# A copy later in ScalarE's queue, fewer warming matmuls, full-height transposes and a narrower update in a linear-attention and two-MoE kernel

## The chip, the cores and the metric

The kernel runs on one core of a Trainium2 chip. The metric is device time in microseconds (us) for one launch. Before the change three runs took 834.9, 834.96 and 835.65 us; the median is 834.96 us.

## What is computed

Three stages follow one another, all in float32 as far as the result can see.

```
state[d,e] = alpha[t,d] * state[d,e] + k[t,d] * v[t,e]     # linear attention with decay, 4 x 8 heads,
y[t,e]     = sum_d q[t,d] * state[d,e]                     # 768 steps, head size 48
x  = y as 3072 tokens x 384
h  = x @ w_in;  x1 = (h * cos(h)) @ w_out                  # first MoE: hidden size 2048
e  = argmax(x1 @ w_gate)                                   # second MoE: 8 experts, hidden size 1024
out[token] = softmax weight * sigmoid(x1 @ w_output_gate)[e] * (relu(x1 @ w1[e]) @ w2[e])
```

## The kernel before

**Attention.** Time is cut into 6 chunks of 128 steps. A unit `u` is one chunk of one batch (`u % 4` is the batch, `u // 4` the chunk), 24 units in all; its 8 heads are kept as 4 pairs. For each unit VectorE (DVE) scans the decays (`decay`, L143, and `recip`, L152), DVE and GpSimd (POOL) scale queries and keys, TensorE (PE) makes scores (L200), transposes the keys (`k_trans`, L211, copied by ScalarE, ACT, in `keys`, L224), applies them to the values (L250, L258) and computes what the chunk adds to the state (`update`, L272; added in `update_out`, L287 and L289). `update` has one matmul for each of the 4 pairs: 112 stationary columns, and 128 moving columns, of which only the first 48 and the last 48 hold values; the 32 between them are zeros of the layout. The profile shows each of these float32 matmuls as two instructions, so 8 for a unit. The units of the last chunk have no update.

**Carry.** `carry(u)` does two things. DVE multiplies the decay total of the chunk before (`wtot`) into `dc` (L184), and then ACT copies the new total into `wtot` (L186). That copy must come after the multiplication, as it overwrites what the multiplication reads. `wtot` of a batch is next read by that batch's next unit, four units on.

**First MoE.** Tokens are handled in 6 groups of 512 (four units each). Each group has 16 blocks of 128 hidden columns; a slot `J` is one block of one group, 96 slots in all. In a slot PE runs `stage1` (9 matmuls, L366), then attention work of other units, then `stage2` of the block two slots earlier (9 matmuls, L405). Between them the block passes ACT `nearest` (L373), DVE `turn` (L379), ACT (L380, L381), DVE `gated` (L384), ACT (L391) and POOL (L392). In the first 16 slots the weights are also unpacked: DVE `narrow` (L334, L339, L343), then ACT and POOL `halves` (L354, L355).

**Order.** All engines run their instructions strictly in the order in which the program writes them. The order is written out by hand: every slot has places A, T, B, P, C and D, and a table says which attention step stands at which place. Place A comes right behind `stage1` and ahead of `nearest`; place C stands behind `stage2`. `carry(u)` stands at place A of slot J+2, ahead of `halves` and `nearest`. Units 5, 6 and 7 have theirs in slots 3, 6 and 9; units 8 to 23 have theirs from slot 17 on. Units 0 to 4 are prepared ahead of the slots, where `carry` is simply written last.

**Start.** While the first loads come in, `warm(22)` gives PE 22 matmuls on a zero tile (L717); `warm(9)` comes later, between the first key transposes and the first values. Both stand in PE's queue ahead of the real work.

**Second MoE.** The rows are sent to buckets by expert in memory and fetched back 448 at a time: three tiles of 128 rows and one of 64 (the first 256 rows of expert 0 are done early, which leaves it 128 and 64). `load_rows` fetches them and sets 10 columns of the 64 missing rows to zero on DVE (L617). `rows_trans` transposes each tile on PE in three pieces of 128 columns (L629), ACT and DVE copy the result out (L630, L631). Experts 1 to 7 take 12 transposes each, in the order 128, 128, 128, 64 rows, three times; it stands among the matmuls of the expert before (L658). In all there are 24 transposes of 64 rows.

Of the kernel before, what the change touches and what calls it, by code (L numbers as in the profile page):

```python
# [8 lines left out]
F32 = mybir.dt.float32  # L9
# [10 lines left out]
B, H, S, D = 4, 8, 768, 48  # L20
DM = H * D
KD = DM // 128
C = 128
# [14 lines left out]
ROW = DM + 10  # L38

QO, KO, AO, VO = 0, 4 * C, 8 * C, 8 * C + 4 * 130 + 8  # L40
UCOL = VO + 4 * C
EARLY = 256
MAGIC = 1.5 * 2.0 ** 23
TWO_PI = 2.0 * math.pi
# [10 lines left out]
def kernel(  # L55
# [11 lines left out]
    nc = tc.nc  # L67
# [6 lines left out]
    ps_a = ctx.enter_context(tc.tile_pool(name="ps_a", bufs=1, space=PSUM))  # L74
    ps_h = ctx.enter_context(tc.tile_pool(name="ps_h", bufs=2, space=PSUM))
    ps_m = ctx.enter_context(tc.tile_pool(name="ps_m", bufs=3, space=PSUM))
# [9 lines left out]
    x_p = m1.enter_context(tc.tile_pool(name="x_p", bufs=1, side="left"))  # L86
# [4 lines left out]
    u_p = at.enter_context(tc.tile_pool(name="u_p", bufs=3, side="right"))  # L91
# [12 lines left out]
    ident = c_sb[:, CI:CI + 128]  # L104
# [7 lines left out]
    wtot = [st_p.tile([128, 4], F32, name=f"wtot{b}") for b in range(B)]  # L112


    un, wt, rc, sc_t, y_t, xt = {}, {}, {}, {}, {}, {}

    def load_unit(u, parts=((0, UCOL),)):
        if u not in un:
            if u == B - 1:

                un[u] = tuple(x_p.tile([128, n], F32, tag=t, name="un") for n, t in ((AO, "xh"), (UCOL - AO, "xl")))
            else:
                t = u_p.tile([128, UCOL], F32, tag="un", name="un")
                un[u] = (t[:, 0:AO], t[:, AO:UCOL], t)
        for c0, c1 in parts:
            t, o = (un[u][2], 0) if len(un[u]) > 2 else (un[u][c0 // AO], c0 // AO * AO)
            nc.sync.dma_start(out=t[:, c0 - o:c1 - o], in_=units[u][:, c0:c1])

    def views(u):
        qk, av = un[u][:2]  # L130
        return (
            qk[:, QO:QO + 4 * C].rearrange("p (a c) -> p a c", a=4),
            qk[:, KO:KO + 4 * C].rearrange("p (a c) -> p a c", a=4),
            wt[u],
            av[:, VO - AO:].rearrange("p (a c) -> p a c", a=4),
        )

    def decay(u):
# [38 lines left out]
    def carry(u):  # L177

        b, i = u % B, u // B
        w = views(u)[2]  # L180
        wb = wtot[b].rearrange("p (a c) -> p a c", c=1)
        if i > 0:
            dc_t[u] = d_p.tile([128, 4, 1], F32, tag="dc", name="dc")
            nc.vector.tensor_tensor(out=dc_t[u], in0=wb, in1=w[:, :, 64:65], op=ALU.mult)  # L184
        if i < NCH - 1:
            nc.scalar.copy(wb, w[:, :, 129:130])  # L186

    def carry_state(u, eng=nc.gpsimd):
        b, i = u % B, u // B
        if i > 0:  # L190
            dc = dc_t.pop(u)
            m = state[b]
            eng.tensor_tensor(out=m, in0=m, in1=dc.to_broadcast([128, 4, 2 * D]), op=ALU.mult)
# [72 lines left out]
    def update(u):  # L266
        if u // B == NCH - 1:
            return
        ks = sc_t[u][1]
        pp = (ps_a if u < B else ps_m).tile([128, 4, C], F32, tag="acc1" if u < B else "m", name="pp")  # L270
        for p in range(4):
            nc.tensor.matmul(  # L272
                out=pp[0:64 + D, p, :], lhsT=ks[:, p, :], rhs=views(u)[3][:, p, :],
                start=True, stop=True,
            )
        pp_t[u] = pp

    def update_out(u):
        b, i = u % B, u // B
        if i == NCH - 1:  # L280
            return
        pp = pp_t.pop(u)
        for p0, c0, v0 in ((0, 0, 0), (64, D, C - D)):
            m = state[b][p0:p0 + D, :, c0:c0 + D]
            pv = pp[p0:p0 + D, :, v0:v0 + D]
            if i == 0:
                nc.scalar.copy(m, pv)  # L287
            else:
                nc.vector.tensor_tensor(out=m, in0=pv, in1=m, op=ALU.add)  # L289
# [316 lines left out]
    def load_rows(e, r0, n, pool, tag):  # L606

        tiles = [min(128, n - o) for o in range(0, n, 128)]
        nt = len(tiles)
        xe = pool.tile([128, nt, ROW], F32, tag=tag, name="xe")  # L610
        full, rest = divmod(n, 128)
        r0 += e * REG
        after_sends(nc.sync.dma_start(
            out=xe[:, 0:full, :], in_=xs[r0:r0 + full * 128, :].rearrange("(j p) c -> p j c", p=128)
        ))
        if rest:
            nc.vector.memset(xe[rest:128, full, DM:ROW], 0.0)  # L617
            after_sends(nc.sync.dma_start(out=xe[0:rest, full, :], in_=xs[r0 + full * 128:r0 + n, :]))
        return dict(e=e, n=n, tiles=tiles, xe=xe)

    def rows_trans(r, pool, th, tl):
        n = r["n"]
        xh = pool.tile([128, KD, n], F32R, tag=th, name="exh")
        xl = pool.tile([128, KD, n], F32R, tag=tl, name="exl")
        for k in range(KD):
            tp = ps_m.tile([128, 512], F32, tag="m", name="tp")[:, :n]
            for j, m in enumerate(r["tiles"]):
                o = j * 128
                nc.tensor.transpose(tp[:, o:o + m], r["xe"][0:m, j, k * 128:(k + 1) * 128], ident[0:m, 0:m])  # L629
            nc.scalar.copy(xh[:, k, :], tp)  # L630
            nc.vector.tensor_tensor(out=xl[:, k, :], in0=tp, in1=xh[:, k, :].bitcast(F32), op=ALU.subtract)  # L631
        r["x"] = (xh, xl)
        r["h"] = {}
# [80 lines left out]
    def warm(n):  # L714
        idle = ps_h.tile([128, 512], F32, tag="h", name="idle")
        for _ in range(n):
            nc.tensor.matmul(out=idle, lhsT=busy[:, 0:128], rhs=busy, start=True, stop=True)  # L717
# [5 lines left out]
    def at_slot(J, place, f, *args):  # L723
        plan.setdefault((J, place), []).append(lambda: f(*args))
# [6 lines left out]
    for u in range(GU, NU):  # L731
        J = NF * (u // GU - 1) + ((-2, 1, 4, 7) if u // GU == 1 else (-1, 2, 5, 7))[u % GU]
        at_unit[u] = J
        if u > GU:

            at_slot(max(J - 6, at_unit[u - 3] + 7 if u - 3 >= GU else 0), "A", load_unit, u)
            at_slot(J, "A", decay, u)
            at_slot(J, "D", q_right, u)
            at_slot(J, "B", recip, u)
            at_slot(J + 1, "D", q_left, u)  # L740
            at_slot(J + 2, "A", k_left, u, nc.vector)
            at_slot(J + 2, "A", k_right, u, nc.vector)
            at_slot(J + 2, "A", carry, u)
            at_slot(J + 2, "D", carry_state, u)
        at_slot(J + 3, "P", scores, u)
        at_slot(J + 3, "C", masked, u, 0)
        at_slot(J + 4, "A", masked, u, 1)
        at_slot(J + 4, "P", k_trans, u)
        at_slot(J + 4, "C", keys, u)
        at_slot(J + 5, "P", values, u)  # L750
        at_slot(J + 5, "C", x_out, u)
        at_slot(J + 6, "P", update, u)
        at_slot(J + 6, "C", update_out, u)
    for g in range(NG - 1):
        J = NF * (g + 1)

        fi = (2, 2, 3)
        tr, n, rn, sd = ((2, 3, 4, 4), 7, 9, 10) if g < NG - 2 else ((2, 3, 4, 5), 5, 7, 8)
# [30 lines left out]

    with tc.manual_schedule():  # L790
        nc.scalar.activation(out=busy[:, 0:1], in_=halfpi, func=ACTF.Sin)
        warm(22)
        load_words(0, 0)
        load_words(0, 1)
        load_words(0, 2)
# [3 lines left out]
        def prepare(u):  # L799
            if u == 0:  # L800
                decay(u)
            q_right(u)
            k_left(u, nc.gpsimd)
            recip(u)
            k_right(u, nc.vector)
            q_left(u, nc.vector)
            carry(u)

        prepare(0)
        scores(0)  # L810
# [46 lines left out]
        k_left(4, nc.vector)  # L857
        k_right(4, nc.vector)
        carry(4)
        carry_state(4, nc.vector)  # L860
        nc.vector.tensor_copy(base, c_sb[:, CEB:CEB + E])
        nc.vector.tensor_copy(tri16, c_sb[:, CT:CT + 128])
# [5 lines left out]
        for J in range(NF * NG):  # L868
            g, j = divmod(J, NF)
# [17 lines left out]
            t = nearest(g, j)  # L887
# [14 lines left out]
    with tc.manual_schedule(engines={ENG.PE, ENG.Activation, ENG.DVE, ENG.SP}):  # L902
# [60 lines left out]
        r = begin(0)  # L963
        rows_trans(r, z_p, "exh", "exl")
        second(7)
        for t in range(n_t):
# [7 lines left out]
            out=nt[:, 0:E], in0=nt[:, 0:E], scalar1=float(127 - CAP), scalar2=127.0, op0=ALU.add, op1=ALU.max  # L974
# [5 lines left out]
        for e in range(E):  # L980
# [8 lines left out]
            for j in range(NEF):  # L989

                n = r["n"]
# [28 lines left out]
            r = nxt  # L1020
# [6 lines left out]
    with tc.If(nov > 0):  # L1027
        with tc.tile_pool(name="ov_p", bufs=1, side="left") as ov_p:
# [13 lines left out]
            for e in range(E):  # L1042
# [6 lines left out]
                with tc.For_i(0, n_e, 1) as it:  # L1049
# [3 lines left out]
                        out=far, in0=far, scalar=float(E * REG), in1=rid, op0=ALU.mult, op1=ALU.add  # L1053
# [4 lines left out]
                        out=xs, out_offset=bass.IndirectOffsetOnAxis(ap=ri, axis=0),  # L1058
# [4 lines left out]
                    tp = ps_m.tile([128, KD, C], F32, tag="m", name="tp")  # L1063
# [3 lines left out]
                    for j in range(NEF):  # L1067
                        hp = ps_h.tile([128, 512], F32, tag="h", name="hp")[:, :C]
                        for k in range(KD):
                            nc.tensor.matmul(  # L1070
                                out=hp, lhsT=f1[:, k, j * 128:(j + 1) * 128], rhs=xT[:, k, :],
# [4 lines left out]
                    for j in range(NEF):  # L1076
                        nc.tensor.matmul(
                            out=op, lhsT=hT[:, j, :], rhs=f2[:, j, :], start=(j == 0), stop=(j == NEF - 1)
# [3 lines left out]
                        out=out, out_offset=bass.IndirectOffsetOnAxis(ap=tk[:, 0, :], axis=0),  # L1082
# [75 lines left out]
```

## Time and profile before

| what | value |
|---|---|
| median of three runs | 834.96 us |
| profiled execution, its own time | 836.24 us |
| its span | 834.5 us |
| granted TensorE clock, mean | 0.987 |
| PE busy | 797.1 us (96%) |
| DVE busy | 500.4 us (60%) |
| ACT busy | 427.3 us (51%) |
| POOL busy | 311.4 us (37%) |

Span and rows are from one profiled execution. A line of a timeline begins with the start and the length in us, then the engine, the line of the kernel, the operation, what it writes and reads, and how many instructions were merged; the bracket at the end is how long the engine stood idle before it and what it waited for. PEld is the load of TensorE's stationary operand, which overlaps with the matmuls. The granted clock is 1.00 at 2.4 GHz and 0.50 at 1.2 GHz.

### The profile page before, as it was taken

What the parts mean: (1) busy time and instruction counts of PE and PEld (TensorE: products, weight loads), DVE (VectorE), ACT (ScalarE), POOL (GpSimd) and SP (SyncE); (2) the same over time, 40 slices, a digit from 0 to 9 for tenths busy, and PEclk for the clock granted to TensorE, in tenths of its full rate; (3) what the DMA queues carried; (4) which work ended last, traced back from release to release, by engine and by line L of the source; (5) the groups of instructions that cost most, each with busy time, mean ns of one, the idle gap of its engine ahead of it and who ended that gap; (6) DMA issues with size and microseconds to landing.
All of it is one profiled execution on the core that took longest, in us unless ns stands there. A gap on an engine that the chain in (4) does not pass through costs nothing.

```text
span 834.5 us, 13942 instructions
## 1 busy us (share of the span) xinstructions
PE 797.1 (96%) x5415; PEld 671.7 (80%) x5415; DVE 500.4 (60%) x968; ACT 427.3 (51%) x782; POOL 311.4 (37%) x284
## 2 busy tenths in 40 slices
PE   8679799999999999999999999999999999999994
PEld 4457577788888888888878878889999999999994
DVE  7989998675467546763766335653764464454530
ACT  2355455754575457644665476564554453453420
POOL 3456557544355336443555333742000100101101
PEclk9998999999999999999999999999999999999998
DMA  9424443723201130123010002304753543533201
GB/s 336 162 98 165 165 165 105 256 59 113 73 2 52 71 122 0 52 70 123 1 52 30 30 1 77 115 1 146 232 160 104 166 140 110 167 123 117 78 11 36
DMA packets 46731, 85.22 MB, mean 102 GB/s; under 512 B 4136, under 2 KB 38216, under 8 KB 44096
## 3 DMA queue, kind: packets, MB, share of 16 engines
q1 hardware_dynamic: 43200, 74.67, 27.5%
q0 software_dynamic: 3456, 9.57, 3.1%
q8 instruction: 45, 0.74, 0.4%
q14 instruction: 30, 0.25, 0.1%
HBM read 69.01 MB, written 15.99 MB: 102 GB/s over the span
## 4 chain that ended last, share of the span: by engine, by line
PE 53%; issue 27%; DVE 10%; POOL 4%; ACT 2%; DMA 1%; POOLq 0%; SPq 0%; ACTq 0%; DVEq 0%
PE acc L405 21%; PE hp L366 21%; POOL out_dram L678 4%; DVE cv L334 2%; PE sc L200 2%; DVE cv L339 2%; PE yp L258 2%; PE yp L250 2%; PE pp L272 1%; DVE cv L343 1%; PE tp L429 1%; DVE t L384 1%; DVE w L143 1%; DVE t L379 1%; PE lp L461 1%
## 5 line engine op out<-in xcount | busy, mean ns | idle before, releaser
L392 POOL TENSOR_TENSOR gl<-t,gh 128x512 fp32r<-128x512 f32 x95 | 126.8, 1335 | 182.3 <-ACT gh L391 140.2
L373 ACT ACTIVATE t<-hp 128x512 f32<-128x512 f32 x96 | 57.3, 597 | 121.5 <-PE hp L366 110.6
L384 DVE TENSOR_TENSOR t<-hp,t 128x512 f32<-128x512 f32 x96 | 65.7, 684 | 88.1 <-ACT t L381 88.1
L379 DVE SCALAR_TENSOR_TENSOR t<-t,hp 128x512 f32<-128x512 f32 x96 | 65.7, 685 | 86.9 <-ACT t L373 86.6
L678 POOL DMA_INDIRECT out_dram<-ot,tk x32 | 30.9, 967 | 220.8 <-ACT ot L677 220.5
L658 PE MATMUL op<-h,hb 128*128 128x384 f32 x384 | 102.8, 340 | 0.0
L648 DVE SCALAR_TENSOR_TENSOR hb<-hp,hb 128x64 fp32r<-128x64 f32 (+3 forms) x136 | 45.3, 372 | 75.4 <-ACT hb L646 75.3
L405 PE MATMUL acc<-gh,woh 128*128 128x512 f32 x288 | 89.1, 416 | 0.0
L366 PE MATMUL hp<-xh,wih 128*128 128x512 f32 x288 | 84.3, 401 | 4.7 <-DVE t L384 2.9
L405 PE MATMUL acc<-gl,woh 128*128 128x512 f32 x288 | 84.4, 400 | 0.0
L405 PE MATMUL acc<-gh,wol 128*128 128x512 f32 x288 | 83.8, 399 | 0.0
L366 PE MATMUL hp<-xh,wil 128*128 128x512 f32 x288 | 83.5, 398 | 0.0
L366 PE MATMUL hp<-xl,wih 128*128 128x512 f32 x288 | 83.4, 398 | 0.0
L380 ACT ACTIVATE t<-t 128x512 f32<-128x512 f32 x96 | 60.7, 632 | 34.8 <-DVE t L379 34.8
L586 DVE TENSOR_TENSOR l<-raw,h 128x768 fp32r<-128x768 f32 x60 | 57.3, 957 | 32.5 <-ACT h L582 31.1
L646 ACT ACTIVATE hb<-hp 128x448 fp32r<-128x448 f32 (+2 forms) x72 | 36.3, 504 | 71.6 <-PE hp L644 71.5
L381 ACT ACTIVATE t<-t,halfpi 128x512 f32<-128x512 f32 x96 | 69.6, 725 | 3.1
L658 PEld LDWEIGHTS op<-h,hb 128*128 128x128 f32 x384 | 69.9, 188 | 0.5
L366 PEld LDWEIGHTS hp<-xh,wih 128*128 128x128 f32 x288 | 54.1, 190 | 19.6 <-DVE t L384 2.0
L366 PEld LDWEIGHTS hp<-xl,wih 128*128 128x128 f32 x288 | 54.7, 190 | 13.4
L405 PEld LDWEIGHTS acc<-gl,woh 128*128 128x128 f32 x288 | 54.7, 190 | 13.2
L366 PEld LDWEIGHTS hp<-xh,wil 128*128 128x128 f32 x288 | 54.5, 189 | 13.2
(139 smaller groups left out, 1501.6 us busy)
## 6 DMA issues: line engine op xcount, KB each, us to landing
raw<-in_w_dram SPq DMA_DIRECT2D x64, 384.0 KB, 3.2
un<-in_units_dram SPq DMA_DIRECT2D x20, 1032.0 KB, 5.1
raw<-in_w_in_dram SPq DMA_DIRECT2D x16, 384.0 KB, 3.6
raw<-in_w_out_dram SPq DMA_DIRECT2D x16, 384.0 KB, 4.0
xs<-zrow SPq DMA_DIRECT2D x8, 591.0 KB, 5.9
xe<-xs SPq DMA_DIRECT2D x7, 591.0 KB, 5.6
un<-in_units_dram SPq DMA_DIRECT2D x4, 512.0 KB, 6.0
un<-in_units_dram SPq DMA_DIRECT2D x4, 264.0 KB, 5.1
```

What stands on the lines that cost most here:

```text
L366: nc.tensor.matmul(out=hp, lhsT=w[:, k, fs], rhs=x[:, k, :], start=(n == 0), stop=(n == 3 * KD - 1))
L373: nc.scalar.activation(out=t, in_=hps[g, j], func=ACTF.Copy, bias=MAGIC)
L379: nc.vector.scalar_tensor_tensor(out=t, in0=t, scalar=MAGIC, in1=hp, op0=ALU.subtract, op1=ALU.subtract)
L380: nc.scalar.activation(out=t, in_=t, func=ACTF.Abs)
L381: nc.scalar.activation(out=t, in_=t, func=ACTF.Sin, scale=-TWO_PI, bias=halfpi)
L384: nc.vector.tensor_tensor(out=t, in0=hps.pop((g, j)), in1=t, op=ALU.mult)
L392: eng.tensor_tensor(out=gl, in0=gf, in1=gh.bitcast(F32), op=ALU.subtract)
L405: nc.tensor.matmul(out=acc[g][k], lhsT=w[:, j, ks], rhs=a, start=(j == 0 and n == 0), stop=(j == NF - 1 and n == 2),)
L586: (nc.vector.tensor_tensor if i < 4 else sub)(out=lo, in0=raws[i], in1=h.bitcast(F32), op=ALU.subtract)
L648: nc.vector.scalar_tensor_tensor(out=out_, in0=hp[:, c], scalar=0.0, in1=hh[:, c].bitcast(F32), op0=ALU.max, op1=ALU.subtract)
L658: nc.tensor.matmul(out=op, lhsT=a[:, sl], rhs=w[:, j, :], start=(j == 0 and i == 0), stop=(j == NEF - 1 and i == 2))
L678: sent = nc.gpsimd.indirect_dma_start(out=out, out_offset=bass.IndirectOffsetOnAxis(ap=tk[0:n, t, :], axis=0), in_=ot[0:n], in_offset=None ...
```

## The change

Four edits in one step.

1. The ACT copy of the decay total leaves `carry` and becomes `carry_keep`, which stands at place C of the same slot. Ahead of the slots it is still written right behind `carry`.
2. `warm(22)` becomes `warm(17)`.
3. `rows_trans` transposes all tiles with all 128 rows and a 128-column identity, and `load_rows` sets the 64 missing rows to zero over all 394 columns.
4. `update` moves only the 96 columns that hold values, by a strided view of two runs of 48; its result is 96 columns wide, and the unit's tile is 32 columns longer so that the view of the last pair stays inside.

```diff
+UPAD = UCOL + C - 2 * D
...
         if i > 0:
             dc_t[u] = d_p.tile([128, 4, 1], F32, tag="dc", name="dc")
             nc.vector.tensor_tensor(out=dc_t[u], in0=wb, in1=w[:, :, 64:65], op=ALU.mult)
+
+    def carry_keep(u):
+        b, i = u % B, u // B
         if i < NCH - 1:
-            nc.scalar.copy(wb, w[:, :, 129:130])
+            nc.scalar.copy(wtot[b].rearrange("p (a c) -> p a c", c=1), views(u)[2][:, :, 129:130])
...
-        pp = (ps_a if u < B else ps_m).tile([128, 4, C], F32, tag="acc1" if u < B else "m", name="pp")
+        pp = (ps_a if u < B else ps_m).tile([128, 4, 2 * D], F32, tag="acc1" if u < B else "m", name="pp")
         for p in range(4):
+            o = VO - AO + p * C
+            v = un[u][1][:, o:o + 2 * (C - D)].rearrange("p (n c) -> p n c", n=2)[:, :, 0:D]
             nc.tensor.matmul(
-                out=pp[0:64 + D, p, :], lhsT=ks[:, p, :], rhs=views(u)[3][:, p, :],
+                out=pp[0:64 + D, p, :], lhsT=ks[:, p, :], rhs=v,
...
-            nc.vector.memset(xe[rest:128, full, DM:ROW], 0.0)
+            nc.vector.memset(xe[rest:128, full, :], 0.0)
...
-            tp = ps_m.tile([128, 512], F32, tag="m", name="tp")[:, :n]
-            for j, m in enumerate(r["tiles"]):
-                o = j * 128
-                nc.tensor.transpose(tp[:, o:o + m], r["xe"][0:m, j, k * 128:(k + 1) * 128], ident[0:m, 0:m])
+            tp = ps_m.tile([128, 512], F32, tag="m", name="tp")
+            for j in range(len(r["tiles"])):
+                nc.tensor.transpose(tp[:, j * 128:(j + 1) * 128], r["xe"][:, j, k * 128:(k + 1) * 128], ident)
+            tp = tp[:, :n]
...
             at_slot(J + 2, "A", carry, u)
+            at_slot(J + 2, "C", carry_keep, u)
...
-        warm(22)
+        warm(17)
```

## Rows read from the trace of the kernel before

**Rows 1.** Windows: stretch, length, busy us (instructions) of each engine, granted clock, DMA.
```profile
10.00:20.00 10.00, 9.36 (x129) 6.82 (x125) 8.34 (x15) 2.87 (x8) 2.00 (x4) 1.00 1.06 389
20.00:30.00 10.00, 7.04 (x110) 5.20 (x108) 9.71 (x19) 3.25 (x9) 2.32 (x3) 1.00 0.77 275
...
80.00:120.00 40.00, 34.36 (x235) 27.02 (x237) 38.25 (x65) 21.20 (x41) 24.32 (x23) 0.96 0.44 157
...
170.00:220.00 50.00, 50.00 (x440) 40.85 (x439) 27.26 (x59) 23.07 (x41) 20.33 (x18) 1.00 0.28 98
...
620.00:670.00 50.00, 50.00 (x270) 46.72 (x269) 23.41 (x47) 21.83 (x38) 7.23 (x8) 1.00 0.45 143
```

**Rows 2.** Timeline of the first 11 us, all engines.
```profile
0.93 0.49 DVE L704 MEMSET scan<- 128x520 f32 x1 [0.93 <-PEq L1147]
...
2.30 7.43 PE L717 MATMUL idle<-busy 128*128 128x512 bf16 x22 [2.30 <-ACT busy L791]
...
7.08 0.89 DVE L165 TENSOR_TENSOR un<-un 128x252 f32<-128x252 f32 x1
7.40 1.84 PEld L717 LDWEIGHTS <-busy 128*128 128x128 bf16 x9 [0.27 <-issue]
...
9.66 1.16 PE L200 MATMUL sc<-un 64*128 64x128 f32 x16
...
10.86 1.29 DVE L219 TENSOR_TENSOR at<-sc,mask 128x512 f32<-128x512 f32 x2 [1.58 <-PE sc L200]
```

**Rows 3.** Timeline around slot 3, all engines.
```profile
53.35 1.01 DVE L343 SCALAR_TENSOR_TENSOR cv<-raw,cv 128x384 uint32<-128x384 uint32 x2
...
55.55 0.15 DVE L184 TENSOR_TENSOR dc<-wtot,w 128x4 f32<-128x4 f32 x1
55.74 0.20 ACT L186 COPY wtot<-w 128x4 f32<-128x4 f32 x1 [3.40 <-DVE dc L184]
...
56.67 0.59 ACT L373 ACTIVATE t<-hp 128x512 f32<-128x512 f32 x1
...
57.29 0.69 DVE L379 SCALAR_TENSOR_TENSOR t<-t,hp 128x512 f32<-128x512 f32 x1 [1.58 <-ACT t L373]
```

**Rows 4.** Timeline of DVE in slot 6.
```profile
79.94 0.69 DVE L379 SCALAR_TENSOR_TENSOR t<-t,hp 128x512 f32<-128x512 f32 x1 [1.59 <-ACT t L373]
```

**Rows 5.** Timeline of PE from 94 to 143 us, where it waits.
```profile
94.79 0.57 PE L211 MATMUL kp<-c_sb,un 112*128 112x112 f32 x4 [2.95 <-DVE state L289]
...
108.89 1.16 PE L200 MATMUL sc<-un 64*128 64x128 f32 x14 [0.39 <-DVE xl L304]
...
114.72 0.57 PE L211 MATMUL kp<-c_sb,un 112*128 112x112 f32 x4 [0.28 <-DVE state L289]
...
142.64 0.97 PE L366 MATMUL hp<-xh,wih 128*128 128x512 f32 x3 [1.51 <-DVE t L384]
```

**Rows 6.** Timeline of PE (an update) and PEld (192-column matmuls).
```profile
254.26 1.03 PE L272 MATMUL pp<-un,ks 128*112 128x128 f32 x8
...
581.54 0.41 PEld L644 LDWEIGHTS hp<-exh,h 128*128 128x128 f32 x3
...
581.88 0.41 PEld L644 LDWEIGHTS hp<-exl,h 128*128 128x128 f32 x3
```

**Rows 7.** Instructions of line 272: count, ns shortest/median/longest, first and last start.
```profile
L272 PE MATMUL pp<-un,ks x160: 270/272/363, 14.2 to 390.1; 128*112 128x128 f32 x160
```

**Rows 8.** Timeline of PE: transposes of three lines, and what follows two.
```profile
249.35 0.88 PE L429 MATMUL tp<-c_sb,xh 128*128 128x128 f32 x6
249.98 0.94 PE L405 MATMUL acc<-gh,woh 128*128 128x512 f32 x3
...
578.36 1.20 PE L629 MATMUL tp<-c_sb,xe 64*128 64x64 f32 x5 [0.29 <-DMA xe<-xs]
...
620.83 2.05 PE L629 MATMUL tp<-c_sb,xe 128*128 128x128 f32 x12
...
622.81 0.45 PE L658 MATMUL op<-h,hb 128*128 128x384 f32 x1
```

More of the change, by code (lines that the diff above doesn't have):

```diff
@@ L119, in load_unit @@
             if u == B - 1:
-                un[u] = tuple(x_p.tile([128, n], F32, tag=t, name="un") for n, t in ((AO, "xh"), (UCOL - AO, "xl")))
+                un[u] = tuple(x_p.tile([128, n], F32, tag=t, name="un") for n, t in ((AO, "xh"), (UPAD - AO, "xl")))
             else:
-                t = u_p.tile([128, UCOL], F32, tag="un", name="un")
-                un[u] = (t[:, 0:AO], t[:, AO:UCOL], t)
+                t = u_p.tile([128, UPAD], F32, tag="un", name="un")
+                un[u] = (t[:, 0:AO], t[:, AO:UPAD], t)
         for c0, c1 in parts:
@@ L134, in views @@
             wt[u],
-            av[:, VO - AO:].rearrange("p (a c) -> p a c", a=4),
+            av[:, VO - AO:UCOL - AO].rearrange("p (a c) -> p a c", a=4),
         )
@@ L282, in update_out @@
         pp = pp_t.pop(u)
-        for p0, c0, v0 in ((0, 0, 0), (64, D, C - D)):
+        for p0, c0 in ((0, 0), (64, D)):
             m = state[b][p0:p0 + D, :, c0:c0 + D]
-            pv = pp[p0:p0 + D, :, v0:v0 + D]
+            pv = pp[p0:p0 + D, :, c0:c0 + D]
             if i == 0:
@@ L807, in prepare @@
             carry(u)
+            carry_keep(u)
         prepare(0)
@@ L859 @@
         carry(4)
+        carry_keep(4)
         carry_state(4, nc.vector)
```

## The prediction

> **What bounds the kernel now.** I read the busy times by stretch first, then who waits for whom, then the timelines around each edit. The stretches show two regimes [rows 1]. From 170 to 220 us PE is busy for all 50.00 us while DVE is busy for 27.26, and from 620 to 670 us the same with 23.41: there a microsecond off PE is a microsecond off the kernel, and one off ACT or DVE is nothing. From 80 to 120 us it is the other way round: DVE is busy for 38.25 of 40 us, PE for 34.36. There DVE sets the pace, and PE stands still until DVE lets a buffer go: 2.95 us at 94.79, 0.39 at 108.89, 0.28 at 114.72 and a last 1.51 at 142.64 [rows 5]. Behind that last wait PE runs without a gap that matters. So edits on the DVE or ACT side count only before 142.64 us, and edits on PE count from there on.
>
> **Part 1, fewer warming matmuls.** The last operand of the first scores is scaled on DVE at 7.08 + 0.89 = 7.97 us, but the scores start at 9.66, because PE is still in its 22 warming matmuls (2.30 + 7.43 = 9.73) [rows 2]. DVE then waits 1.58 us for them before it masks at 10.86. From 7.40 us on nine stationary loads take 1.84 us, the last about 0.15 of it, so one fast matmul is 1.69 / 8 = 0.21 us. Five fewer are 1.05 us. The scores would start at 8.61, still behind 7.97, so all of it counts; masking moves to 9.81, and DVE is nearly full from there (9.71 of 10 us from 20 to 30 [rows 1]). Bounds: 0 if a load holds the chain a little later, 1.69 if DVE's 7.97 were reached. I take 1.05.
>
> **Part 2, the copy.** In slot 3 ACT has nothing to do for 3.40 us, because the copy at 55.74 stands first in its queue and must wait for DVE's `dc` (55.55 + 0.15 = 55.70) [rows 3]. Behind it are two weight casts and `nearest`, which ends at 56.67 + 0.59 = 57.26; DVE's `turn` waits for that, idle for 1.58 us. With the copy at place C, the casts need only `narrow`, which ends at 53.35 + 1.01 = 54.36. From the copy's start to the end of `nearest` it takes 57.26 - 55.74 = 1.52 us; put behind 54.36, even all of that ends at 55.88, and without the copy and with the first cast already done it ends near 55.4. So `turn` starts between 55.72 and 55.9, and at most 0.2 us of the wait is left. Slot 6 shows the same, 1.59 us, and so does slot 9 at 102.55; one row stands for both [rows 4]. In all that is 3 x 1.58 = 4.75 us of DVE time. The copy itself, 0.20 us, now runs where ACT is idle, and nobody is behind it who waits: `wtot` is read four units on. No DMA and no other queue is moved, and for units 0 to 4 the copy keeps its place. From slot 17 on the same ACT waits exist, but PE is full there, so I cost the move at nothing; if PE were not full, up to 1.6 us a unit would be on offer.
>
> How much of 1.05 + 4.75 = 5.8 reaches PE? Up to 94.79 PE waits for DVE by 2.95 us even after its own earlier waits, so the 1.05 + 1.58 + 1.59 = 4.2 gained by then pass whole. The third, at 102.55, is followed only by waits of 0.39 and 0.28 [rows 5]; PE becomes the limit, and DVE then waits for PE's results. At 142.64 DVE is late by 1.51 us once more, but by then its chain has been fed by PE. So parts 1 and 2 together give 4.2 + 0.39 + 0.28 = 4.9; I say 5.0, with the hand-overs around those waits. Bounds: 2.6 (only part 1 and one slot) and 6.6. The upper end is 5.8 and the half of the clock loss: the granted clock of 0.96 from 80 to 120 us [rows 1] means 3.2 us at 1.2 GHz, 1.6 us of work lost behind the 2.95 wait.
>
> **Part 3, the update.** A unit's 8 instructions span 1.03 us [rows 6]; with the last one's own length of 0.27 off [rows 7], 7 intervals are 0.76, or 0.108 us each. If columns alone decided, 96 in place of 128 would save a quarter, 0.027 each and 0.22 a unit. But each instruction also loads its stationary operand. Where only 192 columns move, three loads start every 0.34 us (581.54 to 581.88 [rows 6]), 0.113 us each for 128 stationary columns. Scaled to the update's 112 columns that is 0.099 us, below which the interval can't fall: 0.108 - 0.099 = 0.009, times 8 is 0.07, and with the last instruction's shorter stream 0.08 a unit. Units 8 to 19 run it behind 142.64, 12 of them: 1.0 us. The strided read of two runs of 48 appears nowhere in the trace; if it cost as much as the saving, part 3 is 0, and if it slowed each instruction by a tenth it is -1.0. The other end is 12 x 0.22 = 2.6. I take 1.0, by the row nearest to it in kind, a load-limited matmul.
>
> The Trainium skill ("TensorE: Matmul & The Clock Gate", section "LDWEIGHTS (loading the stationary operand)") gives the load as stationary columns divided by 1.2, in ns, which is 93 ns for 112. By that the interval falls by 0.015 us and part 3 is an estimated 1.4 us; its section "Back-to-back issue gap" has a gap by moving columns alone, which would be the 2.6. The row of 0.113 us speaks for the load.
>
> **Part 4, full-height transposes.** Twelve transposes, nine of 128 rows and three of 64, hold PE from 620.83 until the next matmul at 622.81, 1.98 us [rows 8]. Six of 128 rows in a run hold it for 249.98 - 249.35 = 0.63, or 0.105 each. Twelve of these are 1.26 us, so 0.72 is saved; I take 0.7, since the 0.63 may hide a little in the group behind it. Seven experts: 4.9. Expert 0's five, mixed 128 and 64, span 1.20; less a last one of about 0.27 [rows 7], four intervals are 0.93, and at 0.105 they would be 0.42, so 0.5. Together 5.4, all on a full PE. Bounds: 4.0 (0.5 for each and for expert 0) and 6.4 (0.85 and 0.5). The larger memset has 394 columns; 520 take 0.49 us [rows 2], so it takes 0.37 where 10 columns were set, eight times, on a DVE that is idle half of the time [rows 1] and one expert ahead of its use. For expert 0 it stands right ahead of the transposes, but PE waits there for a DMA anyway. If that cover were gone, it would cost 0.37 once.
>
> **Sum.** 5.0 + 1.0 + 5.4 = 11.4 us. The profiled execution took 836.24 us, span 834.5 and 1.7 around it, which gives 824.8. It stands 1.28 above the median of 834.96, so I predict 834.96 - 11.4 = 823.6 us.
>
> **Rivals.**
> - *PE or ACT swallows the freed DVE time* (chance 0.22). `nearest` is held by the casts or by `stage1`, or POOL's subtractions now fall on `narrow` and slow it. For: the casts still wait for `narrow`. Against: `narrow` ends 1.3 us ahead of `dc`. Then parts 1 and 2 give 2.6: 826.0 us.
> - *The update goes by moving columns* (0.15): part 3 is 2.6, 822.0 us.
> - *Full-height transposes are no cheaper* (0.07). The 64-row ones stream half the columns; if the 1.98 us comes from the copies out of PSUM, 24 transposes grow by half of 0.105, 1.3 us in all: 823.6 + 5.4 + 1.3 = 830.3 us. Against: the three results have a buffer each, and no row has PE waiting for a copy there. The Trainium skill ("TensorEngine Tiling (Array Packing)", section "When to Use Tiling") advises small row tiles for 64 rows; its "Key Properties" say that a change of tile mode drains the engine, which is how I read the 1.98 against 1.26.
> - *Slower: the clock* (0.03). If PE's clock is not up before the 17th matmul ends, the attention start runs at 1.2 GHz. Its 9.36 + 7.04 = 16.4 us of PE work between 10 and 30 us [rows 1] doubles, less the 3.6 us idle: 12.8 us lost and part 1's 1.05 not won, 837.4 us. It decides from a rise later than about 9.5 us; the row has it by 7.40, after 12 matmuls. The skill (first page named, "Part 1") says that the rise comes at another matmul from run to run, which is why I leave a chance.
>
> **Numbers.** The forecast has 0.53. 0.2% is 1.7 us, about what a measurement of this kernel can tell from no change. All the kinder bounds together gain 15.6 us, 819.4; all the unkinder 5.6, 829.4. Not all fall one way, so I give 819.8 to 828.0, which holds the first two rivals and leaves out the other two and the tails. Faster 0.95, within 0.2% 0.02 (a shorter spell at the low clock), slower 0.03.
>
> **What would show it.** Scores at about 8.6 us and masking at 9.8; DVE's `turn` in slots 3, 6 and 9 without its 1.6 us; PE's last wait for DVE at about 137.6 in place of 142.64; a unit's update at about 0.95 us in place of 1.03, with DVE's additions behind it (two of 48 x 192, as before) unchanged; twelve transposes in about 1.3 us. Wrong would be: a new DVE or PE wait of over 1 us before slot 12, an update that is no shorter or a quarter shorter, or transposes that still take 2 us.

## The result, and the profile after

| | before | after |
|---|---|---|
| median, runs side by side | 835.26 us (834.9 to 835.65, 4 runs) | 823.74 us (822.4 to 824.57, 4 runs) |
| profiled execution, its own time | 836.24 us | 823.47 us |
| its span, mean granted clock | 834.5 us, 0.987 | 821.6 us, 0.988 |

The ratio is 0.986, 95% interval [0.9843, 0.9878]: 11.5 us by the medians, 12.8 between the two profiled executions. 823.6 had been predicted. The single terms did less well than their sum, as the runs below show.

**The start.** Timeline of the kernel after, first 10 us.

```profile
5.70 1.68 PEld L725 LDWEIGHTS <-busy 128*128 128x128 bf16 x8 [0.28 <-issue]
...
8.16 1.16 PE L205 MATMUL sc<-un 64*128 64x128 f32 x16 [0.29 <-issue]
```

The scores start 1.50 us earlier than in [rows 2], not 1.05. In this execution the loads come close together (the 2.4 GHz level) from 5.70 us, in the one of before from 7.40; and the scores no longer wait for the warming but for their last operand, which DVE ends at 7.65 + 0.41 = 8.06 us.

**Slot 3.** First the kernel before, in rows not shown yet, then the kernel after. They show DVE's key operations, POOL's subtractions and `narrow`; the last row, DVE's `xl`, is taken here as the end of the slot's work.

```profile
54.88 0.41 DVE L169 TENSOR_TENSOR un<-un,w 128x256 f32<-128x256 f32 x1
...
57.89 2.09 DVE L334 TENSOR_SCALAR cv<-raw 128x384 uint32<-128x384 uint32 x2
58.38 1.40 POOL L392 TENSOR_TENSOR gl<-t,gh 128x512 fp32r<-128x512 f32 x1
...
59.91 1.65 DVE L339 SCALAR_TENSOR_TENSOR cv<-raw,cv 128x384 uint32<-128x384 uint32 x2
...
63.01 0.54 DVE L304 SCALAR_TENSOR_TENSOR xl<-yp,xh 128x384 fp32r<-128x384 f32 x1
```

```profile
52.95 1.02 POOL L362 TENSOR_TENSOR wil<-cv,wih 128x384 fp32r<-128x384 f32 x1 [2.25 <-ACT wih L361]
...
53.32 0.93 DVE L171 TENSOR_TENSOR un<-un,w 128x256 f32<-128x256 f32 x1
...
53.91 1.21 POOL L362 TENSOR_TENSOR wol<-cv,woh 128x384 fp32r<-128x384 f32 x1
54.17 1.24 DVE L175 TENSOR_TENSOR un<-un 128x256 f32<-128x256 f32 x1
55.09 1.46 POOL L399 TENSOR_TENSOR gl<-t,gh 128x512 fp32r<-128x512 f32 x1
55.33 1.24 DVE L186 TENSOR_TENSOR dc<-wtot,w 128x4 f32<-128x4 f32 x1
56.49 0.68 DVE L386 SCALAR_TENSOR_TENSOR t<-t,hp 128x512 f32<-128x512 f32 x1
...
57.09 0.87 DVE L341 TENSOR_SCALAR cv<-raw 128x384 uint32<-128x384 uint32 x2
...
57.88 1.01 DVE L346 SCALAR_TENSOR_TENSOR cv<-raw,cv 128x384 uint32<-128x384 uint32 x2
...
60.36 0.54 DVE L311 SCALAR_TENSOR_TENSOR xl<-yp,xh 128x384 fp32r<-128x384 f32 x1
```

`turn` (L386) has lost its wait of 1.58 us [rows 3], but the three key operations ahead of it have grown from 0.41, 0.41 and 0.15 us to 0.93, 1.24 and 1.24. Each ends right behind an operation of POOL: POOL's end at 53.97, 55.12 and 56.55 us, DVE's at 54.25, 55.41 and 56.57. The old copy had held up the casts, and with them POOL; now POOL subtracts while DVE scales keys. (The copy itself runs at 58.87 without a wait.) In exchange the first two operations of `narrow` (L341), which had run beside POOL for 2.09 us, take 0.87, and the next two (L346) 1.01 instead of 1.65. At the last row of each fence the kernel after is 2.65 us ahead, against 1.56 at the first key operation: the slot has won 1.1, not 1.58. And it won this behind `turn`, not ahead of it: from the first key operation to `turn` it takes 3.17 us where it took 2.41, and from `turn` to the last row 3.87 where it took 5.72.

Slots 6 and 9 do the same and win 1.1 each (there too the key operations take 0.93, 1.22 to 1.23 and 1.25). Slot 5 gives 0.5 back, as its `narrow` lies beside POOL for longer. Before, then after:

```profile
73.78 1.35 DVE L334 TENSOR_SCALAR cv<-raw 128x384 uint32<-128x384 uint32 x2
```

```profile
71.11 1.85 DVE L341 TENSOR_SCALAR cv<-raw 128x384 uint32<-128x384 uint32 x2
```

**Where PE waits for DVE.** Timeline of PE in the kernel after.

```profile
91.49 0.57 PE L216 MATMUL kp<-c_sb,un 112*128 112x112 f32 x4 [1.39 <-DVE state L296]
...
104.49 1.16 PE L205 MATMUL sc<-un 64*128 64x128 f32 x14 [0.94 <-DVE xl L311]
...
138.25 0.97 PE L373 MATMUL hp<-xh,wih 128*128 128x512 f32 x3 [1.61 <-DVE t L391]
```

The wait of 2.95 us [rows 5] is down to 1.39, at 91.49 in place of 94.79, a lead of 3.30 us. The next ends at 104.49 instead of 108.89, a lead of 4.40. The last one ends at 138.25 instead of 142.64: 4.39 us won by then, where 5.0 was said. On DVE the same sum is 1.56 us at slot 3, three slots of 1.1 each, less the 0.5.

**Slot 17.** Before, then after: ACT's copy and the conversion behind it, and PE's transposes.

```profile
146.83 0.20 ACT L186 COPY wtot<-w 128x4 f32<-128x4 f32 x1 [1.66 <-DVE dc L184]
...
149.57 1.55 ACT L418 ACTIVATE xh<-acc 128x512 f32<-128x512 f32 x3
...
151.18 0.33 PE L429 MATMUL tp<-c_sb,xh 128*128 128x128 f32 x1 [0.16 <-ACT xh L418]
```

```profile
144.40 1.56 ACT L425 ACTIVATE xh<-acc 128x512 f32<-128x512 f32 x3
...
145.82 0.55 PE L436 MATMUL tp<-c_sb,xh 128*128 128x128 f32 x3
```

The copy had kept the conversion to `xh` late here, and PE fed its three transposes one by one. Now they run together, and `stage2` follows at 146.12. The lead grows from 4.41 us to 5.14, where nothing had been counted.

**Update and transposes.** Timeline of PE, and the group of line 279 (count, ns shortest/median/longest), kernel after.

```profile
248.75 0.93 PE L279 MATMUL pp<-un,ks 128*112 128x96 f32 x8
...
L279 PE MATMUL pp<-un,ks x160: 243/262/337, 12.7 to 383.7; 128*112 128x96 f32 x160
```

```profile
613.57 1.47 PE L636 MATMUL tp<-c_sb,xe 128*128 128x128 f32 x12
614.79 0.42 PE L666 MATMUL op<-h,hb 128*128 128x384 f32 x1
```

A unit's update is 0.93 us against 1.03 [rows 6]; an interval is (0.93 - 0.262) / 7 = 0.095 us. By the end of the first MoE the lead is 6.34 us, so the update gave 1.2. Twelve transposes hold PE for 614.79 - 613.57 = 1.22 us against 1.98 [rows 8]: 0.76 each time. The lead at the end is 12.8.

The shape of the stages is as it was: from 80 to 120 us DVE is still full (39.35 of 40), and from 620 to 670 us PE is (50.00 of 50).

### The profile page after: what moved, and what is told of

Its sections match the earlier page's. It is cut to its first block, busy times and chain, and to the rows that moved or that the text cites. A ratio compares the mean times of both kernels' runs of the same rounds, so it can differ in the third digit from the quotient of the medians.

```text
span 821.6 us, 13914 instructions
## 1 busy us (share of the span) xinstructions
PE 786.0 (96%) x5410; PEld 669.2 (81%) x5410; DVE 503.7 (61%) x968; ACT 425.3 (52%) x782; POOL 312.2 (38%) x284
## 4 chain that ended last, share of the span: by engine, by line
PE 54%; issue 26%; DVE 11%; POOL 4%; DMA 1%; ACT 1%; POOLq 0%; SPq 0%; ACTq 0%; DVEq 0%
PE acc L412 22%; PE hp L373 21%; POOL out_dram L686 4%; PE sc L205 2%; DVE cv L341 2%; PE yp L263 2%; PE yp L255 2%; DVE cv L346 2%; DVE cv L350 1%; PE pp L279 1%; PE tp L436 1%; DVE t L391 1%; DVE w L145 1%; DVE t L386 1%; PE lp L468 1%
## 5 line engine op out<-in xcount | busy, mean ns | idle before, releaser
L386 DVE SCALAR_TENSOR_TENSOR t<-t,hp 128x512 f32<-128x512 f32 x96 | 65.7, 684 | 79.5 <-ACT t L380 79.1
L373 PE MATMUL hp<-xh,wih 128*128 128x512 f32 x288 | 83.9, 399 | 3.5 <-DVE t L391 2.9
L373 PE MATMUL hp<-xh,wil 128*128 128x512 f32 x288 | 83.5, 398 | 0.0
L373 PE MATMUL hp<-xl,wih 128*128 128x512 f32 x288 | 83.4, 398 | 0.0
L373 PEld LDWEIGHTS hp<-xh,wih 128*128 128x128 f32 x288 | 54.1, 190 | 18.4 <-ACT woh L361 2.1
L412 PEld LDWEIGHTS acc<-gh,wol 128*128 128x128 f32 x288 | 54.9, 191 | 13.0
L373 PEld LDWEIGHTS hp<-xl,wih 128*128 128x128 f32 x288 | 54.6, 190 | 13.3
```

Source lines behind the costliest of these rows:

```text
L373: nc.tensor.matmul(out=hp, lhsT=w[:, k, fs], rhs=x[:, k, :], start=(n == 0), stop=(n == 3 * KD - 1))
L386: nc.vector.scalar_tensor_tensor(out=t, in0=t, scalar=MAGIC, in1=hp, op0=ALU.subtract, op1=ALU.subtract)
L412: nc.tensor.matmul(out=acc[g][k], lhsT=w[:, j, ks], rhs=a, start=(j == 0 and n == 0), stop=(j == NF - 1 and n == 2),)
```

## The experiments

The first four are the parts alone, each made from the kernel before.

**1. The copy alone.**

```diff
...
+            at_slot(J + 2, "C", carry_keep, u)
...
```

> The copy moved to place C alone, the rest as before. Theory A (the changed kernel's trace read as it stands): DVE's wait of 1.58 us in slots 3, 6 and 9 goes, but about half of it comes back as longer DVE operations beside POOL, so 1.1 to 1.5 us of three waits of 1.58 reach PE in all about 2.9; and PE's stop at the first row transposes of slot 17 (0.73 us, from 150.24 to 151.27 in the kernel before) goes too, because ACT is free earlier there. Together 3.6 us faster, ratio about 0.9957. Theory B (the prediction): 3.95 us at the start and nothing from slot 17 on, ratio about 0.9953, with the stop in slot 17 still there. The trace tells them apart, the time does not.

Measured: 832.95 us against 835.94; ratio 0.996 [0.9945, 0.9975], 3.3 us (2.1 to 4.6). Two rows of its timeline, `turn` of slot 3 and the transposes of slot 17:

```profile
57.27 0.68 DVE L382 SCALAR_TENSOR_TENSOR t<-t,hp 128x512 f32<-128x512 f32 x1
...
146.07 0.55 PE L432 MATMUL tp<-c_sb,xh 128*128 128x128 f32 x3
```

No wait ahead of `turn`, and its key operations are at 0.93, 1.24 and 1.24 us as well. The stop in slot 17 is gone with the copy alone; in the kernels of experiments 2 and 4, where the copy has not moved, it is still there (0.16 us idle ahead of the third transpose). So both effects are the copy's.

**2. Seventeen warming matmuls alone.**

```diff
-        warm(22)
+        warm(17)
```

> 17 warming matmuls in place of 22, the rest as before. Prediction: five fast matmuls of 0.21 us less, 1.05 us faster, ratio 0.9987, scores at 8.6 us. Rival: the changed kernel had its scores at 8.16, 1.5 us earlier; if that comes from fewer matmuls and not from an earlier rise of the clock in that execution, the scores start at 8.16 here again and the ratio is 0.9982. Other rival: DVE's later waits swallow it, ratio 1.000.

Measured: 835.95 us; ratio 1.0006 [0.9988, 1.0024]: nothing that can be told from no change. The start in its trace:

```profile
5.27 1.88 PEld L717 LDWEIGHTS <-busy 128*128 128x128 bf16 x9 [0.28 <-issue]
...
8.23 1.16 PE L200 MATMUL sc<-un 64*128 64x128 f32 x16 [0.59 <-POOL un L169]
```

The clock was up at 5.27 us here, and the scores waited 0.59 us for an operand. The profile puts the wait down to POOL's, but that one was done at 7.00 + 0.86 = 7.86 us; DVE's was the last, at 7.24 + 0.89 = 8.13. In experiment 1, with 22 matmuls and the clock up at 5.16, the scores start at 8.49. With an early clock the edit is worth about 0.3 us. With a late one it is worth what the prediction said: in the kernel of experiment 9, also with 17 matmuls, the clock was up at 7.36 us, and the scores start 1.1 us earlier than the 9.66 of [rows 2].

```profile
7.36 0.75 PEld L725 LDWEIGHTS <-busy 128*128 128x128 bf16 x4 [0.24 <-issue]
...
8.54 1.16 PE L205 MATMUL sc<-un 64*128 64x128 f32 x16
```

**3. The transposes alone.**

```diff
...
-                nc.tensor.transpose(tp[:, o:o + m], r["xe"][0:m, j, k * 128:(k + 1) * 128], ident[0:m, 0:m])
+                nc.tensor.transpose(tp[:, j * 128:(j + 1) * 128], r["xe"][:, j, k * 128:(k + 1) * 128], ident)
...
```

> Full-height transposes and the wider zero alone, the rest as before. Prediction: 0.7 us for each of seven experts and 0.5 for expert 0, 5.4 us, ratio 0.9935. Rival, from the trace after: 0.76 us each and 1.1 around expert 0, 6.5 us, ratio 0.9922. If the gain came from another part of the change, the ratio is near 1.000.

Measured: 829.06 us; ratio 0.9916 [0.9898, 0.9933], 7.0 us. Twelve transposes hold PE for 1.22 us in its trace too.

**4. The update alone.** The edit is the one of `update` and `update_out` shown above.

> The update on 96 columns alone, the rest as before. Load theory: 0.11 us a unit (span of the eight instructions 1.03 to 0.93 us) in 12 units, 1.2 to 1.3 us faster, ratio 0.9985. Column theory: 0.22 a unit, 2.6 us, ratio 0.9969. The four parts alone should add up to the 11.5 us of the whole change within 1 us if they do not depend on each other.

Measured: 835.52 us; ratio 0.9992 [0.998, 1.0004], 0.7 us with zero inside the interval. By the ratios the four alone come to 3.3 - 0.5 + 7.0 + 0.7 = 10.5 us, where the whole gave 11.5 by the medians. Each of the four is uncertain by 1 us or more, so they add up as far as can be told.

**5. Transposes of 64 rows, grouped** (from the kernel before): first the nine of 128 rows, then the three of 64.

```diff
...
+        for want in (128, 64):
+            for k in range(KD):
+                for j, m in enumerate(r["tiles"]):
+                    if m == want:
...
```

> The kernel before, but with the transposes of one expert in another order: first the nine of 128 rows, then the three of 64, each of 64 rows as before. If the change of the row tile is what costs (once there and back for each of three pieces), two of three changes go: the twelve take about 1.4 to 1.5 us in place of 1.98, and seven experts gain 3.5 to 4 us, ratio 0.9955. If a 64-row transpose is slow by itself, the twelve still take 1.98 us and the ratio is 1.000. The copies out of PSUM start later here, which nobody should wait for.

Measured: 832.15 us against 835.43; ratio 0.9957 [0.9945, 0.9968]. Timeline:

```profile
620.28 1.47 PE L631 MATMUL tp<-c_sb,xe 128*128 128x128 f32 x12
621.68 0.44 PE L662 MATMUL op<-h,hb 128*128 128x384 f32 x1
```

1.40 us in place of 1.98, with the same twelve instructions in another order. The height of a transpose costs little; the change of height does. The old order has six changes from 128 rows to 64 or back, the grouped one two: (1.98 - 1.40) / 4 = 0.15 us for each.

**6. An update with 64 columns.** It moves two runs of 32 instead of 48, and so leaves out a third of the update.

```diff
...
-            v = un[u][1][:, o:o + 2 * (C - D)].rearrange("p (n c) -> p n c", n=2)[:, :, 0:D]
+            v = un[u][1][:, o:o + 2 * (C - D)].rearrange("p (n c) -> p n c", n=2)[:, :, 0:32]
...
```

> The changed kernel, but the update moves only 64 of the 96 columns (two runs of 32); the other third of what a chunk adds to the state is left out. Load theory (the stationary load of 112 columns sets the interval): the eight instructions still start about 0.095 us apart and a unit's span stays at 0.91 to 0.93 us. Column theory: the interval falls by a third to 0.06 us, the span to 0.7 us.

Measured (one run): 824.72 us. Timeline:

```profile
250.07 0.91 PE L279 MATMUL pp<-un,ks 128*112 128x64 f32 x8
```

A third fewer columns, and the interval goes only from 0.095 to (0.91 - 0.262) / 7 = 0.093 us. From 96 columns on, the moving columns no longer set it. What is left is the load of the 112 stationary columns; that it sets the interval is the likely reading, but no run changed their number.

**7. Slots 3, 6 and 9 without POOL's two subtractions.** ACT writes plain copies in their place, later in the slot. The low halves of those weights are then no longer right, and this kernel does other work later on (one run, 935.41 us), so only the trace of the slots counts and not the time.

```diff
...
-        nc.gpsimd.tensor_tensor(out=lo, in0=f, in1=hi.bitcast(F32), op=ALU.subtract)
+            plan.setdefault((late, "T"), []).append(lambda: nc.scalar.copy(lo, f))
...
```

> The changed kernel, but in slots 3, 6 and 9 the low halves of the weights are not computed on POOL; ACT writes plain copies behind `nearest` instead, so POOL is free of those two subtractions. If DVE's key scaling and dc (0.93, 1.24 and 1.24 us in slot 3, where the kernel before has 0.41, 0.41 and 0.15) were stretched by POOL running at the same time, they go back to 0.41, 0.41 and 0.15, unless the next POOL subtraction falls on them, and `turn` starts about 2 us earlier. If the stretch came from ACT or from the clock of DVE, they stay long.

Measured, DVE and POOL in slot 3:

```profile
53.36 0.41 DVE L171 TENSOR_TENSOR un<-un,w 128x256 f32<-128x256 f32 x1
...
54.03 0.15 DVE L186 TENSOR_TENSOR dc<-wtot,w 128x4 f32<-128x4 f32 x1
...
54.52 1.30 POOL L402 TENSOR_TENSOR gl<-t,gh 128x512 fp32r<-128x512 f32 x1 [3.77 <-issue]
54.70 2.23 DVE L341 TENSOR_SCALAR cv<-raw 128x384 uint32<-128x384 uint32 x2
```

The key operations are back at 0.41, 0.41 and 0.15 us: it was POOL that held them. But `narrow` now meets POOL's next subtraction and takes 2.23 us instead of 0.87. The slot's last step is at 59.33 instead of 60.36: a lead of 1.0 us, from 2.4 us less of key operations and 1.4 us more of `narrow`. PE's last wait for DVE (L376 here) ends at 136.40 instead of 138.25.

**8. Unit 4's copy later as well** (from the kernel after): its `carry_keep` goes to place C of slot 0.

> The changed kernel, with unit 4's copy, which still stands ahead of `nearest` in front of slot 0, moved to place C of slot 0. Theory: ACT's wait of 4.9 us there goes, `nearest` and the key copy of unit 3 run about 3 us earlier, PE's stop of 4.0 us ahead of the update of unit 3 (35.40 in the changed kernel) falls below 1.5 us, and PE does not fall to 1.2 GHz behind it. DVE is nearly full there, so the kernel gains only DVE's wait in slot 1, 0.3 to 0.5 us: ratio to the changed kernel 0.9995, to the kernel before about 0.986. Rival: PE runs ahead and the low clock moves to a place where it costs, up to 1.6 us slower.

Measured: 823.86 us against 835.43; ratio 0.986 [0.9843, 0.9876], the same as the kernel after. Timeline of PE:

```profile
32.62 1.03 PE L279 MATMUL pp<-un,ks 128*112 128x96 f32 x8 [0.72 <-ACT ks L229]
...
39.32 0.94 PE L373 MATMUL hp<-xh,wih 128*128 128x512 f32 x3 [2.45 <-DVE scan L144]
```

The first wait, 3.96 us in the kernel after, is 0.72 here, and comes back as waits for DVE: a new one of 2.45, and one of 2.58 at 47.56 where the kernel after has 1.32. PE, waiting less for ACT, only reaches DVE's limit sooner; its last wait for DVE ends at 137.94.

**9. Key operations away from POOL** (from the kernel after): for units 5 to 7 they stand behind `narrow`.

```diff
...
+        if j in (3, 6, 9):
+            for f in (k_left, k_right):
+                at_slot(j, "B", f, 4 + j // 3, nc.vector)
+            at_slot(j, "B", carry, 4 + j // 3)
...
```

> The kernel after the change, with the three key operations and the carry of units 5 to 7 moved from place A of slots 3, 6 and 9 to place B, behind `narrow`. Theory (DVE loses time only where POOL's wide subtractions run beside it): the key operations now fall where POOL is nearly idle and return to about 0.41, 0.41 and 0.15 us, `turn` starts some 2.4 us earlier, but the first operations of `narrow` fall beside POOL and take about 2.1 to 2.2 us for the two instead of 0.87 (as in the kernel before and in the run without POOL's subtractions). DVE's time of a slot falls by 0.6 to 1.2 us; PE waits for DVE through these slots, so the first group of slots gains 0 to 3 us: 821 to 824 us, ratio to the kernel before 0.982 to 0.986. Rival (the length of DVE's work does not depend on POOL, the key operations are slow for their own operands): they stay 0.93, 1.24 and 1.24 us at their new place, the scores of units 5 to 7 come later than now, and the time is 824 to 828 us.

Measured: 824.79 us against 836.5; ratio 0.9852 [0.9825, 0.9879]. Slot 3, POOL and DVE, then PE's waits up to 145 us (total, times, longest), of this kernel and of the kernel after:

```profile
55.85 2.05 DVE L341 TENSOR_SCALAR cv<-raw 128x384 uint32<-128x384 uint32 x2
...
56.29 1.40 POOL L399 TENSOR_TENSOR gl<-t,gh 128x512 fp32r<-128x512 f32 x1
...
59.70 0.41 DVE L171 TENSOR_TENSOR un<-un,w 128x256 f32<-128x256 f32 x1
...
PE kp L216 <- DVE state L296: 6.6, 3, 3.6
...
PE sc L205 <- issue: 2.5, 1, 2.5
...
PE sc L205 <- DVE scan L144: 0.6, 1, 0.6
```

```profile
PE sc L205 <- DVE scan L144: 5.4, 2, 3.9
...
PE kp L216 <- DVE state L296: 1.7, 2, 1.4
```

The theory's rows came as said: the key operations are short where POOL is idle, and `narrow` is long beside POOL. Slot 3 is 0.7 us shorter by it (54.10 to 61.04, where the kernel after has 52.72 to 60.36). The time did not move all the same: PE waits less ahead of the scores (L205), 0.6 and 2.5 us in place of 5.4, and more ahead of the key transposes (L216), 6.6 in place of 1.7. Its last wait for DVE ends at 140.41, 2.16 us behind the kernel after; at 48.69, ahead of slot 3, it was 1.39 behind already. The rival (operations slow by themselves) is out. No order tried beats the kernel after by more than the interval.

**10. Two warming matmuls** (from the kernel after).

```diff
-        warm(17)
+        warm(2)
```

> The kernel after the change with `warm(2)` in place of `warm(17)`. It tests the price of the rival in which the clock stays at 1.2 GHz through the attention's start. By the prediction's price for that rival (the PE work of the first 40 us at half speed where it bounds) the time is up to 13 us longer: up to 837 us, with a granted clock near 0.5 from the first scores on. By the other theory (the start is bound by the loads, DVE and ACT, and PE has slack there) the clock is as low, PE's rows of the first 20 us are twice as long, and the time is 0 to 4 us longer: 824 to 828 us.

Measured: 826.92 us; ratio 0.988 [0.9852, 0.9909]. Timeline of the start:

```profile
8.01 2.08 PE L205 MATMUL sc<-un 64*128 64x128 f32 x16 [4.67 <-DVE scan L144]
...
12.53 0.80 PEld L725 LDWEIGHTS <-busy 128*128 128x128 bf16 x4 [0.28 <-issue]
```

The scores take 2.08 us instead of 1.16, the rate of the 1.2 GHz level, and the loads close up at 12.53. The values start at 13.76 against 11.73, and PE's last wait for DVE (L373) ends at 141.46 against 138.25. So this colder start costs 3.2 us in the profile and 1.7 by the two ratios, whose intervals overlap; not 13. The clock was up again at 12.53 us, during `warm(9)`; a start that stays at 1.2 GHz up to 30 us, as the prediction priced it, did not occur in any run.

**11. The wide zeroing alone** (from the kernel before).

```diff
-            nc.vector.memset(xe[rest:128, full, DM:ROW], 0.0)
+            nc.vector.memset(xe[rest:128, full, :], 0.0)
```

> The kernel before with one part of the transposes' edit alone: the 64 missing rows are set to zero over all 394 columns, the transposes stay as before. Every other expert's first stage (72 matmuls of 448 columns) takes 14.88 us before and 14.59 us after the change, at the same granted clock and with the same instructions. If the zeroed rows (or the DVE work that zeroes them) are the cause, that stage takes 14.59 us here; if the transposes with 64 rows are, it stays at 14.88 us. The 12 transposes stay at 1.98 us, and the total within 1 us of the kernel before.

Measured (one run): 837.55 us. Timeline of PE, first matmul of a first stage and what follows the stage:

```profile
664.41 0.78 PE L644 MATMUL hp<-exh,h 128*128 128x448 f32 x3
...
679.29 0.34 PE L666 MATMUL op<-h,hb 128*128 128x384 f32 x1
```

679.29 - 664.41 = 14.88 us, as in the kernel before, where the kernel after has 14.59. So the zeroed rows are not the cause. It is 14.59 with the transposes' edit alone, and 14.88 in the kernel of experiment 5, where the 64-row transposes are grouped. It goes with having transposes of 64 rows at all. All 72 matmuls share the difference, about 4 ns each, at the same granted clock of 1.00; by what way the transposes do this to matmuls that come microseconds later stays open.

## Why the prediction was right, and where it wasn't

- **What bounds which stretch: right.** DVE to the last wait at 138.25 us, PE behind it. Experiment 8 took a wait for ACT away and got it back as waits for DVE. Experiment 9 shortened DVE's work in slot 3 but brought the keys later, and PE waited behind them. Experiment 7 shortened DVE's work there and left the order as it was, and that last wait ended 1.85 us earlier.
- **Part 1 (1.05 us): right for the execution it was read from, off for others.** It took the clock's rise at 7.40 us as fixed. The twelve traces with 17 or 22 warming matmuls have it anywhere from 4.84 to 8.25: up to 6.12 in six of them, from 7.36 on in the other six. With a rise at 7.36 to 7.41 the scores start at 9.63 and 9.66 us with 22 matmuls, and at 8.53 to 8.63 with 17: 1.0 to 1.1 us, as priced; with an early one the operands, ready for a start near 8.2, set them, and 0.3 us is left. By the median of experiment 2 it can't be told from nothing.
- **Part 2 (3 x 1.58 = 4.75 us of DVE): the wait went as said, but what it gave came by another way.** The wait ahead of `turn` is gone entirely. But the prediction took the key operations at their old 0.97 us and did not ask what the earlier casts would start. POOL's subtractions came forward with them and held each key operation until they were done: 2.44 us more ahead of `turn`, against 1.58 of wait removed. That the slot won 1.1 all the same is due to `narrow`, which no longer runs beside POOL and is 1.86 us shorter; the prediction had not counted on that. Each of the three slots won 1.1 in place of 1.58, and slot 5 gave 0.5 back. The rival that POOL's subtractions now fall on DVE's work was half right: it is the key operations that meet them, while `narrow` gets faster. The Trainium skill has the rule, "SBUF — State Buffer", section "Who interferes with whom": a DVE instruction with two inputs in SBUF contends with a GpSimd instruction that reads SBUF, the ports that the two share are an exclusive lock, and the order of issue decides who blocks. The trace agrees: each key operation starts behind POOL's start and ends 0.28, 0.29 and 0.02 us behind POOL's end. The kernel before shows it too: the scaling that [rows 2] has at 7.08 us takes 0.89 us beside POOL and ends 0.27 behind it, and a later one of the same size takes 0.41.

```profile
6.84 0.86 POOL L169 TENSOR_TENSOR un<-un,w 128x256 f32<-128x256 f32 x1
...
13.91 0.41 DVE L165 TENSOR_TENSOR un<-un 128x252 f32<-128x252 f32 x1
```

- **Parts 1 and 2 together:** 5.0 was said, 4.39 came by the last wait in the profile. The prediction let 4.2 us through by 94.79 and then only 0.67 of the third slot, as PE would become the limit. It was 3.30, and then the third slot's 1.1 passed whole: the wait of 0.39 ahead of the scores [rows 5] did not go but grew to 0.94, so DVE was still the limit there.
- **"From slot 17 on I cost the move at nothing": wrong by 0.73 us.** A full PE was taken as cover. It hid the late ACT work in most slots, but not where PE's next work was the transposes of that late result.
- **Part 3 (1.0 us): right.** The lead grew by 1.2 us in the profile, and experiment 4 alone gave 0.7, not told from zero. That moving columns don't set the interval below 96, experiment 6 shows; that the load does fits the size: scaling a row of 128 stationary columns gave 0.099 us, the trace has 0.095 at 96 columns and 0.093 at 64. The 93 ns that the load rule of the Trainium skill gave ("TensorE: Matmul & The Clock Gate", section "LDWEIGHTS (loading the stationary operand)") is the better figure. The prediction gave that page's section "Back-to-back issue gap" too narrowly: the formula by moving columns stands there for a single matmul, and the section itself says that in a stream the load and the matmul set the spacing together.
- **Part 4 (5.4 us): the mechanism was right, the size was small.** 6.5 us came: 0.76 for each of seven experts instead of 0.7, which is 5.3; expert 0's 0.5 was lost again, since its transposes waited longer for their DMA (0.89 us against 0.22 and 0.29 for the two tiles) and its first stage for DVE (0.19 and 0.78 against 0.55); and 0.29 us in every other expert, four of the seven, from the unexplained first stage. That the change of height was the cost, experiment 5 shows.
- **The slower rival (the clock, 837.4 us): overpriced, as far as tested.** It doubled PE's work of 20 us. In experiment 10 the clock was low when the scores ran, but up again at 12.53 us, during the second warming, and the cost was 1.7 to 3.2 us.

So the sum was helped by luck: parts 1 and 2 fell 0.6 short, and 0.7 at slot 17 and 1.1 in the transposes stood against it in the profile. Within part 2 it was luck once more, as a shorter `narrow` paid for the longer key operations. The profiles are 12.8 us apart, the medians 11.5. The clock's rise, late before and early after, makes up 0.4 to 0.5 of that: the scores came 1.50 us earlier where the edit gives 1.0 to 1.1 with a late rise in both. What the rest is, no run settles.

## What to carry to other kernels

Before costing a removed wait, list what the freed engine starts earlier and on whose ports that lands: a copy that blocked ACT's queue had been keeping POOL off DVE's key operations. Where instructions of two tile heights alternate on TensorE, pad or group them; where fewer moving columns leave the interval between matmuls as it is (0.095 us at 96, 0.093 at 64 here), look at the load of the stationary operand before cutting more. And a stretch that is bound by one engine's work gives nothing for moving the waits of the others about. A size read from one execution holds for others only if what it hangs on, here the moment of the clock's rise, is the same there.

## What the hardware showed that was not expected

- A 4-column multiplication on DVE takes 0.15 us alone and 1.24 beside a POOL subtraction; a 256-column one 0.41 and 0.93 to 1.24; the first two operations of `narrow` 0.87 with little of POOL beside them, and 2.05 to 2.23 beside its subtractions.
- A change between transposes of 128 and of 64 rows costs about 0.15 us.
- TensorE's rate at the start doubles at a moment that differs from one execution to the next, from 4.84 to 8.25 us in twelve traces with the warming of 17 or 22 matmuls. The column of the granted clock reads 1.00 from 0 to 10 us all the same (in the kernels of experiments 9 and 10 and in the kernel after), also where the scores take 2.08 us: there the lengths tell the level, not the column.
- With 64-row transposes in the program, every other expert's 72 matmuls of 448 columns take 14.88 us instead of 14.59. The cause is open.
